# Layer 1's first product for the last 1536 tokens as seven products over halves of tokens

## The chip, the cores and the metric

The kernel runs on one core of a Trainium2 chip. The metric is device microseconds from the start to the end of one execution; lower is better. The matrix engine is TensorE (PE), the vector engine VectorE (DVE), the activation engine ScalarE (ACT); SyncE (SP) issues all DMA transfers, GpSimd (POOL) does next to nothing here. Each engine works through its own instructions in program order and waits on semaphores for the others.

## The reference

Attention with a causal window of 64 keys (4 batches, 8 heads, 576 positions, head size 64), then two layers over the 2304 tokens, 512 wide with 2048 hidden units, all in float32:

```python
scores = scale * np.matmul(q, k.transpose(0, 1, 3, 2))
mask = (rel >= 0) & (rel < window)          # window = 64
scores = np.where(mask, scores, -1000000000.0)
...
attn = attn / (np.sum(attn, axis=-1, keepdims=True) + 1e-09)
x = np.matmul(attn, v)                      # 2304 tokens x 512
h = np.maximum(x @ w_in, 0.0)               # layer 1: 512 x 2048
x = h * h @ w_out                           #          2048 x 512
h = x @ w_in2                               # layer 2
out = (h * np.cos(h)) @ w_out2
```

## The kernel before

Every float32 matrix is split into a high part, rounded to PE's fast 32-bit type (fp32r), and a low part, the rest. Each product is then three matmuls: high by high, high by low, low by high. W1 and W2 arrive as whole float32 numbers ("raw" transfers of 1 MB, one for each slice of 128 hidden units, with the matching rows of w_out) and are unpacked and split on ACT and DVE (`convert_w`, `convert_w2`). The slices of W1 stay in SBUF; those of W2 go to DRAM as w2a, w2b and w2o and are streamed back.

The tokens are cut into nine parts of 256. Attention for a part n and a half of the heads g gives four blocks of matmuls on PE, in this order: scores S (L556), the transposes T (L593, behind mask and minimum on DVE, exp on ACT and the division on DVE), and the product with v, O (L607). From O come the high part of X on ACT (L643) and the low part on DVE (L646).

Layer 1 takes the parts in units: 512 tokens (first in two halves of 256), 256 tokens, and three times 512 tokens. For a unit and a slice of 128 hidden units, `g1` makes the first product, ph: 12 matmuls (four blocks of 128 input columns, three passes) over the unit's tokens. ACT takes relu of it into r, and the square's high part into g; ACT or DVE squares r; DVE takes the low part (L701). `g2` makes the second product from g: 12 matmuls into four accumulators accA (L715), which stay in PSUM over the 16 slices. After the last slice they are copied and stored to DRAM.

Layer 2 takes 768 tokens at a time, and its first product is already made by the scheme that the change brings to layer 1 (Strassen's in Winograd's form): seven products of 6 matmuls over 384 columns in place of eight, in PSUM tiles x, y and z (L997). Its blocks alternate with the second product, accB (L955). `held` is a product copied out by ACT (L1013), which DVE adds to the next (L1020).

The order of the instructions on each engine is not written by hand. Every step is handed to a planner, `op`, with its engines, a key (its place in the program), the steps it depends on, and the buffers that it takes and uses; its modelled duration is also given. The planner runs a list schedule over these numbers and so fixes the order. SP's transfers are such steps too (`dma`), in one queue.

## Time and profile before

| | |
|---|---|
| median of 3 runs | 872.78 us (869.89 to 873.73) |
| profiled execution | 872.92 us |
| its span, first to last instruction | 871.1 us |
| PE, DVE, ACT busy | 847.9, 572.3, 522.9 us |
| moved by DMA | 144.16 MB, mean 165 GB/s |
| mean granted PE clock | 0.992 |

The profile is of one execution, and its span is 1.8 us shorter than the time. A PE matmul is recorded with a modelled end, and matmuls overlap, so the mean duration of a record is longer than the distance between two of them. Weight loads have an engine row of their own, PEld.

### The profile page before, as it was taken

How to read it: one execution, taken by the hardware profiler on the slowest of the kernel's cores; microseconds unless marked ns; L12 is line 12 of the kernel's file. 1: busy time of each engine (PE TensorE's matmuls, PEld its weight loads, DVE VectorE, ACT ScalarE, POOL GpSimd, SP SyncE). 2: the span in 40 equal slices, each digit the busy share in tenths (PEclk: the TensorE clock that was granted, in tenths of full speed). 3: DMA queues.
4: the chain of work that ended last, by engine and by line, in shares of the span. 5: the costliest groups of instructions: out<-in, count | busy, mean ns of one | idle time of the engine just before them, and what ended most of it. 6: DMA issues, size and time to landing. Idle time of an engine off the chain costs nothing.

```text
span 871.1 us, 13901 instructions
## 1 busy us (share of the span) xinstructions
PE 847.9 (97%) x5232; PEld 737.2 (85%) x5232; DVE 572.3 (66%) x1345; ACT 522.9 (60%) x1101; POOL 5.0 (1%) x25
## 2 busy tenths in 40 slices
PE   5799999999999999999999999999999999999998
PEld 4689788998878887888888899988999988999986
DVE  4977855645756366562731588887688877788851
...
DMA packets 28451, 144.16 MB, mean 165 GB/s; under 512 B 3040, under 2 KB 3552, under 8 KB 18144
## 3 DMA queue, kind: packets, MB, share of 16 engines
...
## 4 chain that ended last, share of the span: by engine, by line
PE 91%; DVE 4%; ACT 3%; DMA 1%; issue 0%; ACTq 0%; DVEq 0%
PE accB L955 23%; PE ph L1106 21%; PE accA L715 19%; PE x L997 12%; PE z L997 6%; PE y L997 3%; PE S L556 2%; PE O L607 2%; PE accA L776 2%; PE T L593 2%; ACT pb L575 1%; DMA w2o_dram<-w2o 1%; ACT raw_in_w_dram L286 0%; DVE pb L585 0%; DVE xr L820 0%; DMA qk<-in_qk_dram 0%
## 5 line engine op out<-in xcount | busy, mean ns | idle before, releaser
L1106 PE MATMUL ph<-X,W_in_w_dram 128*128 128x512 f32 (+1 forms) x1032 | 223.0, 363 | 2.7 <-ACT X L643 1.4
L1106 PEld LDWEIGHTS ph<-X,W_in_w_dram 128*128 128x128 f32 x1032 | 173.7, 193 | 32.5 <-issue 1.5
L715 PE MATMUL accA<-g,W_in_w_dram 128*128 128x512 f32 (+1 forms) x888 | 200.2, 370 | 0.2 <-DVE g L701 0.2
L715 PEld LDWEIGHTS accA<-g,W_in_w_dram 128*128 128x128 f32 x888 | 153.4, 189 | 27.6 <-issue 0.7
L701 DVE TENSOR_TENSOR g<-r,g 128x512 fp32r<-128x512 f32 (+1 forms) x86 | 51.8, 603 | 118.1 <-ACT r L696 117.6
L955 PE MATMUL accB<-wo,gb_e 128*128 128x512 f32 x432 | 100.8, 390 | 0.0
L955 PEld LDWEIGHTS accB<-wo,gb_e 128*128 128x128 f32 x432 | 80.9, 188 | 16.2
L692 ACT ACTIVATE g<-r 128x512 fp32r<-128x512 f32 (+1 forms) x86 | 48.2, 561 | 73.2 <-PE accA L715 71.7
L688 ACT ACTIVATE r<-ph 128x512 f32<-128x512 f32 (+1 forms) x86 | 45.1, 524 | 53.6 <-PE ph L1106 51.7
L575 ACT ACTIVATE pb<-pb,mm 128x128 f32<-128x128 f32 x144 | 55.8, 389 | 11.5 <-DVE mm L569 11.4
L955 PE MATMUL accB<-wo,gb_a 128*128 128x512 f32 x216 | 60.8, 394 | 0.0
L955 PE MATMUL accB<-wo,gb_b 128*128 128x512 f32 x216 | 60.6, 393 | 0.0
L696 ACT ACTIVATE r<-r 128x512 f32<-128x512 f32 (+1 forms) x84 | 47.1, 561 | 2.6
L1013 ACT ACTIVATE held<-x 128x384 f32<-128x384 f32 x72 | 34.6, 480 | 20.1 <-PE x L997 20.0
L997 PE MATMUL x<-X,wa 128*128 128x384 f32 x216 | 46.0, 339 | 0.0
L997 PE MATMUL x<-X,wb 128*128 128x384 f32 x216 | 45.5, 336 | 0.0
L955 PEld LDWEIGHTS accB<-wo,gb_b 128*128 128x128 f32 x216 | 39.9, 188 | 5.6
L997 PEld LDWEIGHTS x<-X,wa 128*128 128x128 f32 x216 | 39.0, 188 | 4.5
L955 PEld LDWEIGHTS accB<-wo,gb_a 128*128 128x128 f32 x216 | 39.6, 188 | 3.7
L905 ACT ACTIVATE u_b<-rr_b,hpi 128x384 f32<-128x384 f32 x24 | 14.8, 617 | 44.9 <-DVE rr_b L901 44.8
L997 PEld LDWEIGHTS x<-X,wb 128*128 128x128 f32 x216 | 38.9, 188 | 2.2
L929 DVE TENSOR_TENSOR gb_e<-keep,gb_e 128x384 fp32r<-128x384 f32 x48 | 25.7, 553 | 21.3 <-ACT gb_e L249 21.3
...
## 6 DMA issues: line engine op xcount, KB each, us to landing
raw_in_w_dram<-in_w_dram SPq DMA_DIRECT2D x32, 1024.0 KB, 5.9
wa<-w2a_dram SPq DMA_DIRECT2D x24, 1024.0 KB, 8.2
...
w2o_dram<-w2o SPq DMA_DIRECT2D x8, 1024.0 KB, 4.3
w2a_dram<-w2a SPq DMA_DIRECT2D x8, 1024.0 KB, 4.4
wo<-w2o_dram SPq DMA_DIRECT2D x8, 1024.0 KB, 11.8
```

Source lines behind the costliest of these rows:

```text
L556: nc.tensor.matmul(S[e][HALF[c], r, i], t["qk"][HALF[e], r, q0:q0 + WINDOW], t["qk"][HALF[e], r, UA + q0:UA + q0 + P], start=(r == 0 and i ...
L575: nc.scalar.activation(t["pb"][:, e, r, i], t["pb"][:, e, r, i], AF.Exp, bias=t["mm"][:, e, r, i:i + 1], scale=-1.0, accum_out=t["sm"][:, ...
L688: nc.scalar.activation(t["r"], ph()[:, 0:w], AF.Relu)
L692: nc.scalar.activation(t["g"][:, 0], t["r"], AF.Square)
L696: nc.scalar.activation(t["r"], t["r"], AF.Square)
L701: nc.vector.tensor_tensor(t["g"][:, 1], t["r"], f32(t["g"][:, 0]), ALU.subtract)
L715: nc.tensor.matmul(self.acc[i][:, k, :], w[:, 1, wl, m * P:m * P + P], t["g"][:, gl, :], start=(j == 0 and p == 0 and k == 0 and self.n > ...
L929: nc.vector.tensor_tensor(t["g"][:, 1], r(), f32(t["g"][:, 0]), ALU.subtract)
L955: nc.tensor.matmul(acc[0], t["g"][:, gl, m * P:m * P + P], wb.tile[:, k % 2, wl], start=(k == 0 and i == 0), stop=(k == NJ - 1 and i == 2))
L997: nc.tensor.matmul(ps[bank], wb.tile[:, i, wl, c * P:c * P + P], piece(o, c, xl), start=(first and c == 0 and k == 0), stop=(last and c == ...
L1013: return b, op({"ACT": act_us(H)}, key - 6, lambda e: nc.scalar.activation(r_at(b), ps[bank], AF.Copy), [dep, o_rooms], [b], [buf], lat=0.39)
L1106: nc.tensor.matmul(t["ph"][:, 0:u.w], wb.tile[:, 0, wl, c * P:c * P + P], u.x(xl, c), start=(c == 0 and k == 0), stop=(c == NCC - 1 and k ...
```

## The change

For the last three units (1536 tokens) the first product is no longer made slice by slice. The tokens of a unit are halved (256 and 256), the 512 input columns are halved, and two slices of 128 hidden units form the two halves of the output: a 2 by 2 by 2 block product, made by seven products of 6 matmuls over 256 columns (`group1`). The order in a group is B11 into x, B21 into y, T2 into x, T1 into the other half of y, T3 into x, T4 into x, B22 into y. Between them stand the eight blocks of three matmuls of 512 columns (`tiles1`) that make the second product of the group before: one behind y, one behind T2, two behind T3, four behind B22. ACT copies x out three times (`hold`, r1 to r3); DVE makes the sums o_11, o_22 and o_12 (`add`); o_21 is a copy on ACT. `act1` then makes relu and square in one DVE operation for both tokens' halves of a slice, the high part on ACT, the low part on DVE.

The seven sums of X for a unit are made by `prepare1`: four differences, seven high parts (ACT or DVE) and seven low parts (DVE), all of 512 columns. The seven pieces have one buffer each and are written again for the next unit. The attention of these units leaves O as a plain float32 copy. The seven weight matrices of each pair of slices are made by `sum_w1` when W1 is unpacked, and stored to DRAM as w1s (1.84 MB for a pair); each group loads its pair again (`load_in1`, in two transfers, w_in), issued when the group two before has ended. A slice of W1 is now split with two operations of 512 columns on each engine and not one of 1024. The conversions of W2 move: four slices behind `sum_w1`, then two with each of the groups 1, 4, 7, 11, 14 and 18. Layer 2's first loads wait for the last load of w_in. In the planner the price of a DMA byte, and for parts from 2 on those of the mask step and of exp, are lower.

```diff
-        return op({"SP": max(0.6 * n, nbytes / 360e3)}, key, fn, [*deps, *order], take, use, lat=2.2)
+        return op({"SP": max(0.6 * n, nbytes / 400e3)}, key, fn, [*deps, *order], take, use, lat=2.2)
...
+            hi = op({"ACT": act_us(DM)}, key, c5, [o4, w_hi[j - 1][k] if q else None],
+                    [] if q else [wb], [rb, wb] if q else [rb])
+            his.append(hi)
+            los.append(op({"DVE": dve_us(DM)}, key, c6, [hi], use=[rb, wb]))
+        w_hi[j], w_lo[j] = his, los
...
+    def sum_w1(i, key, after):
...
+        def s1(e):
+            t["s"] = wp.tile([P, 4, 2, Q], F32R, tag=f"W{sb.slot}", name=f"w1s_{i}")
+            nc.vector.tensor_tensor(raw(1), part(1, 0), part(1, 1), ALU.add)
...
+        def s2(e):
+            nc.vector.tensor_tensor(raw(0), raw(1), part(0, 0), ALU.subtract)
...
+        def s3(e):
+            nc.vector.tensor_tensor(raw(2), part(0, 0), part(1, 0), ALU.subtract)
...
+        def s4(e):
+            nc.vector.tensor_tensor(raw(3), part(0, 1), raw(0), ALU.subtract)
...
+        def lo(e):
+            nc.vector.tensor_tensor(
+                t["s"][:, :, 1], f32(t["s"][:, :, 1]), f32(t["s"][:, :, 0]), ALU.subtract)
...
+        o = op({"DVE": dve_us(2 * DM)}, key, whole, [*ready, after, *cv_last], [ab], [wb])
+        o = op({"DVE": dve_us(Q)}, key, s1, [o], [sb], [ab])
+        o = op({"DVE": dve_us(Q)}, key, s2, [o], use=[ab, sb])
+        o = op({"DVE": dve_us(Q)}, key, s3, [o], use=[ab, sb])
+        o = op({"DVE": dve_us(Q)}, key, s4, [o], use=[ab, sb])
+        cv_last[:] = [o]
+        o = op({"ACT": act_us(4 * Q)}, key, hi, [o], use=[sb])
+        o = op({"DVE": dve_us(4 * Q)}, key, lo, [o], use=[sb])
...
+        w1_stored[i] = [
+            dma(key, whole_st, P * 4 * Q * 4, [*ready, after], use=[wb], n=2),
+            dma(key, st22, P * 2 * Q * 4, [*ready, after], use=[wb]),
+            dma(key, st_a, P * 6 * Q * 4, [o], use=[sb]),
+            dma(key, st_b, P * 2 * Q * 4, [o], use=[sb])]
...
-                    prev = op({"DVE": 0.36}, k_e, lambda q, e=e, r=r, i=i: neg_max(q, e, r, i),
+                    prev = op({"DVE": 0.36 if n < 2 else 0.22}, k_e, lambda q, e=e, r=r, i=i: neg_max(q, e, r, i),
...
-                    ex.append(op({"ACT": 0.59}, k_e, lambda q, e=e, r=r, i=i: exp(q, e, r, i),
+                    ex.append(op({"ACT": 0.59 if n < 2 else 0.39}, k_e, lambda q, e=e, r=r, i=i: exp(q, e, r, i),
...
+            def raw(eng):
...
+                copy(eng, rx(g, th), t["O"].rearrange("p r q -> p (r q)"))
...
+    def prepare1(u, key):
...
+        def sub(dst, a, b, deps):
+            return op({"DVE": dve_us(2 * UA)}, key, lambda e: nc.vector.tensor_tensor(
+                dst(), a(), b(), ALU.subtract), deps, use=d)
...
+        x11, x12, x21, x22 = at(0, 0), at(0, 1), at(1, 0), at(1, 1)
+        a = split1(u, B11, x11, [got[0, 0]], key, d, free(B11))
+        b = split1(u, B21, x21, [got[1, 0]], key, d, free(B21))
+        t1 = sub(x11, x12, x11, [*a, got[0, 1]])
+        s1 = split1(u, T1, x11, [t1], key, d, free(T1))
+        t3 = sub(x12, x22, x12, [t1, got[1, 1]])
+        s3 = split1(u, T3, x12, [t3], key, d, free(T3))
+        s5 = split1(u, B22, x22, [got[1, 1]], key, d, free(B22))
+        t2 = sub(x22, x22, x11, [t1, t3, *s5])
+        s2 = split1(u, T2, x22, [t2], key, d, free(T2))
+        t4 = sub(x21, x21, x22, [t2, *b])
+        s4 = split1(u, T4, x21, [t4], key, d, free(T4))
...
+        def sq(e):
+            nc.vector.scalar_tensor_tensor(r["r"], r["r"], 0.0, r["r"], ALU.max, ALU.mult)
...
+        o = op({"DVE": dve_us(512)}, key, sq, ready, use=[rb[0]])
+        h = op({"ACT": act_us(512)}, key, hi, [o], [gb], [rb[0]])
+        l = op({"DVE": dve_us(512)}, key, lo, [h], use=[rb[0], gb])
...
+    def load_in1(u, i, key, after):
...
+                nc.sync.dma_start(f32(b.tile[:, 0:n]), w1s[i][:, a:a + n])
+
+            o = dma(key, ld, P * n * 2 * Q1 * 4, [*w1_stored[i], *after],
+                    [b, slot] if fresh else [b], [] if fresh else [slot])
...
+    def group1(u, i, key, fill):
...
+        gaps = [[], fill[0:1], fill[1:2], fill[2:4], fill[4:]]
...
+                    for n, (wl, xl) in enumerate(((0, 0), (0, 1), (1, 0))):
+                        nc.tensor.matmul(
+                            out(), wb.tile[:, k, wl, c * P:c * P + P],
+                            piece1(o, xl)[:, c * UA:c * UA + UA],
+                            start=(new and n == 0), stop=(last and c == 1 and n == 2),
...
+
+                line[0] = op({"PE": 3 * pe_us(UA)}, key, mm,
+                             [line[0], o_w, *ready1[u, o], *(deps if c == 0 else ())],
+                             [buf] if new else [], [wb, *s_buf] if new else [wb, buf, *s_buf],
...
+        def hold(dep):
+            b = R["R1"].buf()
+            return b, op({"ACT": act_us(UA)}, key - 6, lambda e: nc.scalar.activation(
+                r_at(b), ps["x"], AF.Copy), [dep], [b], [bx, rr_buf], lat=0.39)
...
+        def add(k, h, r, deps):
+            first = not rows[k][0].users
+            return op({"DVE": dve_us(UA)}, key - 6, lambda e: nc.vector.tensor_tensor(
+                new_r(k)[:, h * UA:(h + 1) * UA], ps["y"][:, h], r_at(r), ALU.add), deps,
+                [rows[k][0]] if first else [], [by, r, rr_buf] + ([] if first else [rows[k][0]]))
...
+        nm = f"{u}_{i}"
+        o = product(0, pa, 0, B11, True, True)
+        r1, o_r1 = hold(o)
+        o = product(1, pa, 1, B21, True, True)
+        o_11 = add(0, 0, r1, [o, o_r1])
+        between()
+        between()
+        o = product(0, pa, 2, T2, False, True, [o_r1])
+        r2, o_r2 = hold(o)
+        between()
+        oz = product(2, pa, 3, T1, True, True, [o_11])
+        o = product(0, pb, 0, T3, False, True, [o_r2])
+        r3, o_r3 = hold(o)
+        o_22 = add(1, 1, r3, [oz, o_r3])
+        between()
+        o = product(0, pb, 1, T4, False, True, [o_r3])
+        o_21 = op({"ACT": act_us(UA)}, key - 3, lambda e: nc.scalar.activation(
+            new_r(1)[:, 0:UA], ps["x"], AF.Copy), [o, o_22], use=[bx, rows[1][0]])
+        gb = act1(key - 3.0, rows[1], [o_22, o_21], f"{nm}b")
+        o = product(2, pb, 2, B22, False, True, [o_22])
+        o_12 = add(0, 1, r2, [o, o_r2, o_11])
+        ga = act1(key - 2.9, rows[0], [o_11, o_12], f"{nm}a")
+        between()
+        return ga, gb
...
+        ends = []
+        for i in range(NJP):
...
+            load_in1(u, i, key - 7.0, ends1[-2:-1])
+            if u * NJP + i in (1, 4, 7, 11, 14, 18):
+                for _ in range(2):
+                    convert_w2(w2_next, key + 8.0, line[0])
+                    w2_next += 1
+            ga, gb = group1(u, i, key, fill)
+            ends1.append(line[0])
+            fill = [*tiles1(u, 2 * i + 1, key + 2.0, gb, i == 0, False, ends),
+                    *tiles1(u, 2 * i, key + 2.0, ga, False, i == NJP - 1, ends)]
+        if u + 1 < NU1:
+            prepare1(u + 1, base1 + 2.0 * (u + 1) * NJP - 2.0)
```

The first place where the order moves is PE's row at the start of the first group. Names are tile<-tiles read: X is the split input, g the split square, accA_0 the accumulators of the 256-token unit ahead. Before, the next unit's products of 512 columns begin between the last second products of that unit:

```order
L715 MATMUL accA_0_1697<-g_2250,W_in_w_dram_1075 128x256 x6
L715 MATMUL accA_1_1733<-g_2250,W_in_w_dram_1075 128x256 x6
L1106 MATMUL ph_2321<-X,W_in_w_dram_370 128x512 x12
L715 MATMUL accA_0_1697<-g_2281,W_in_w_dram_1165 128x256 x6
...
L715 MATMUL accA_0_1697<-g_2325,W_in_w_dram_1229 128x256 x6
L715 MATMUL accA_1_1733<-g_2325,W_in_w_dram_1229 128x256 x6
...
L1106 MATMUL ph_2418<-X,W_in_w_dram_430 128x512 x12
L715 MATMUL accA_0_2449<-g_2355,W_in_w_dram_370 128x512 x3
```

After the change the seven products stand there; between the first y and T2 lie half a fill and eight rows of S, of which one is shown:

```order
L820 MATMUL accA_0_1818<-g_2378,W_6_1136 128x256 x6
L820 MATMUL accA_1_1831<-g_2378,W_6_1136 128x256 x6
L1431 MATMUL x_0_0_2455<-X,w_in_0_0_1674 128x256 x6
L1431 MATMUL y_0_0_2466<-X,w_in_0_0_1674 128x256 x6
L820 MATMUL accA_0_1818<-g_2410,W_7_1247 128x256 x3
L648 MATMUL S_0_0_2481<-qk_0_2039 64x128 x2
...
L1431 MATMUL x_0_0_2455<-X,w_in_0_0_1674 128x256 x6
L820 MATMUL accA_0_1818<-g_2410,W_7_1247 128x256 x3
L1431 MATMUL y_0_0_2466<-X,w_in_0_0_1674 128x256 x6
L1431 MATMUL x_0_0_2455<-X,w_in_0_4_1946 128x256 x6
L820 MATMUL accA_1_1831<-g_2410,W_7_1247 128x256 x6
L1431 MATMUL x_0_0_2455<-X,w_in_0_4_1946 128x256 x6
```

The first product of the unit, ph with 12 matmuls of 512 columns, has given way to x and y with 6 of 256; T2 is the third product row (the second x), T1 the second y, and the second products of the 256-token unit are now the fills.

The second place is DVE just ahead of it. held_1741 and x_raw hold the plain O of the four quarters of X, w2o, w2a and w2b are W2's sums. Before, the low part of X came straight from O, and this stretch had no such rows. After:

```order
L806 TENSOR_TENSOR g_2378<-r_2359,g_2378 128x256
L258 CAST w2o_2357<-cw_in_w_dram_2364 128x512
L428 TENSOR_TENSOR w2o_2357<-cw_in_w_dram_2364,w2o_2357 128x512
...
L428 TENSOR_TENSOR w2b_2422<-cw_in_w_dram_2326,cw_in_w_dram_2364 128x256
L806 TENSOR_TENSOR g_2410<-r_2395,g_2410 128x256
...
L428 TENSOR_TENSOR w2a_2408<-w2a_2408 128x2x256
L927 TENSOR_TENSOR X<-held_1741,X 128x512
L948 TENSOR_TENSOR held_1741<-held_1741,x_raw 128x512
L258 CAST X<-held_1741 128x512
L927 TENSOR_TENSOR X<-held_1741,X 128x512
...
L927 TENSOR_TENSOR X<-held_1741,X 128x512
L1462 TENSOR_TENSOR r_0_0_0_2510<-y_0_0_2466,held_1741 128x256
```

Between the split g_2378, which PE reads ahead of the group, and the low part of T2 (the second row with L927) stand the conversion of a pair of W2's slices, another split of a square, and the difference T2 = x22 - x11 (L948); o_11 (L1462) comes behind the pieces of T4.

The third place is SP in the first groups. Before, the queue held raw slices, q/k, v and the stores of W2's sums:

```order
L275 DMA raw_in_w_dram_3459<-in_w_dram 128x2048
L541 DMA v_1_3494<-in_v_dram 128x1024
L537 DMA qk_0_3544<-in_qk_dram 128x1152
L275 DMA raw_in_w_dram_3596<-in_w_dram 128x2048
L541 DMA v_0_3664<-in_v_dram 128x1024
L372 DMA w2o_dram<-w2o_3547 128x2048
```

After, the pairs of loads of w_in stand between them:

```order
L1370 DMA w_in_0_0_1674<-w1s_dram 128x2048
L1370 DMA w_in_0_4_1946<-w1s_dram 128x1536
L629 DMA qk_0_2938<-in_qk_dram 128x1152
L278 DMA raw_in_w_dram_2954<-in_w_dram 128x2048
L278 DMA raw_in_w_dram_2975<-in_w_dram 128x2048
L1370 DMA w_in_1_0_2075<-w1s_dram 128x2048
L1370 DMA w_in_1_4_2211<-w1s_dram 128x1536
L633 DMA v_0_3071<-in_v_dram 128x1024
L629 DMA qk_1_3090<-in_qk_dram 128x1152
L446 DMA w2o_dram<-w2o_3130 128x2048
L1370 DMA w_in_0_0_1674<-w1s_dram 128x2048
L1370 DMA w_in_0_4_1946<-w1s_dram 128x1536
```

Each pair of loads that moved in is 1.05 and 0.79 MB, and is queued behind the raw slices, q/k, v and stores ahead of it.

## Rows read from the trace of the kernel before

**Rows 1.** The page, busy time of each engine (share of the span), instructions:

```profile
PE 847.9 (97%) x5232; PEld 737.2 (85%) x5232; DVE 572.3 (66%) x1345; ACT 522.9 (60%) x1101; POOL 5.0 (1%) x25
```

**Rows 2.** Waits of PE, whole run: total us, times, longest.

```profile
PE T L593 <- DVE pb L585: 5.2, 5, 2.9
PE T L593 <- ACT pb L575: 4.7, 3, 2.3
PE S L556 <- DMA qk<-in_qk_dram: 4.5, 1, 4.5
```

**Rows 3.** Waits of PE from 50 us to the end.

```profile
PE T L593 <- DVE pb L585: 0.4, 2, 0.2
PE accA L715 <- DVE g L701: 0.2, 1, 0.2
```

**Rows 4.** Windows: us, each engine's busy time, granted PE clock, DMA share, GB/s.

```profile
core 0: us, PE busy (x) PEld busy (x) DVE busy (x) ACT busy (x) POOL busy (x), PEclk, DMA share, GB/s
15.60:49.70 34.10, 25.17 (x277) 21.29 (x278) 28.16 (x73) 29.04 (x65) 0.00 (x0) 0.87 0.86 346
...
111.00:198.60 87.60, 87.37 (x813) 78.76 (x812) 50.37 (x155) 57.03 (x157) 0.00 (x0) 1.00 0.42 153
198.60:486.20 287.60, 287.44 (x1728) 234.49 (x1728) 147.24 (x379) 165.31 (x349) 0.00 (x0) 1.00 0.47 176
505.00:520.00 15.00, 15.00 (x79) 13.93 (x78) 12.43 (x27) 9.42 (x18) 0.00 (x0) 1.00 1.02 425
510.00:579.00 69.00, 69.00 (x361) 64.15 (x360) 59.96 (x128) 41.40 (x80) 0.00 (x0) 1.00 0.51 207
```

**Rows 5.** Groups by line and shape: busy us, mean ns of a record.

```profile
L1106 PE MATMUL ph<-X,W_in_w_dram 128*128 128x512 f32 x696 | 173.3, 395 | 0.0
...
L1106 PE MATMUL ph<-X,W_in_w_dram 128*128 128x256 f32 x336 | 49.7, 297 | 2.7 <-ACT X L643 1.4 <-ACT r L688 1.0 <-DVE X L646 0.3
...
L1013 ACT ACTIVATE held<-x 128x384 f32<-128x384 f32 x72 | 34.6, 480 | 20.1 <-PE x L997 20.0
```

**Rows 6.** Chain that ended last, from 440 us: start, us, what.

```profile
442.87 2.72 PE ph L1106 x12
```

**Rows 7.** The same chain, 60 to 90 us.

```profile
64.81 1.44 PE ph L1106 x12
...
80.51 2.75 PE ph L1106 x12
83.26 1.43 PE accA L776 x12
```

**Rows 8.** The same chain in layer 2, from 506 us.

```profile
506.00 1.39 PE accB L955 x6
507.39 1.04 PE x L997 x6
...
517.55 1.39 PE accB L955 x6
```

**Rows 9.** DVE in time, from 202 us: start, us, instruction.

```profile
202.28 0.42 DVE L354 TENSOR_TENSOR w2b<-cw_in_w_dram,cw_in_w_dram 128x256 f32<-128x256 f32 x1 [1.97 <-DMA w2o_dram<-w2o]
202.62 0.42 DVE L354 TENSOR_TENSOR w2b<-cw_in_w_dram,w2a 128x256 f32<-128x256 f32 x1
...
204.35 0.68 DVE L701 TENSOR_TENSOR g<-r,g 128x512 fp32r<-128x512 f32 x1
204.95 0.68 DVE L354 TENSOR_TENSOR w2b<-w2b 128x512 fp32r<-128x512 f32 x1
```

**Rows 10.** DVE groups by shape: the split of a W1 slice.

```profile
L324 DVE TENSOR_TENSOR W_in_w_dram<-raw_in_w_dram,W_in_w_dram 128x1024 fp32r<-128x1024 f32 x16 | 19.6, 1223 | 7.8 <-ACT W_in_w_dram L249 7.6
```

**Rows 11.** The chain from 198 us: the block S.

```profile
206.95 1.03 PE S L556 x32
```

**Rows 12.** DMA issues from 505 to 520 us: count, KB each, median us to landing.

```profile
wa<-w2a_dram SPq DMA_DIRECT2D x3, 1024.0 KB, 19.8
```

**Rows 13.** Window from 60 to 70 us, columns as in Rows 4.

```profile
60.00:70.00 10.00, 10.00 (x86) 10.00 (x85) 7.99 (x10) 9.90 (x17) 0.00 (x0) 1.00 0.25 79
```

More of the change, by code (lines that the diff above doesn't have):

```diff
@@ L672, in x @@
         def x(self, hl, c):
-            return X[:, self.half, hl, c, self.sl]
+            return (x_first() if self.n == 0 else x_third())[:, hl, c]
         def x_ready(self, c):
@@ L1182 @@
     for jp in range(2):
[L1183 to L1189 removed]
+        load_in(0, jp, base - 8.0 + 2.0 * jp, [*loaded, *w2_end])
+    load_out(0, base - 7.0, [*loaded, *w2_end])
+    gate = loaded[0]
+    fills = [fill[0:4], fill[4:8]]
     job_ends = []
```

322 lines of the change are left out of this document (249 added, 73 removed).

## The prediction

> **What bounds the kernel now.** I read the busy times first. TensorE (PE) is busy 847.9 of 871.1 us [rows 1], so the reader is to see that only two things can move the time: the work that PE has, and the 23 us in which it waits. The waits come next: three kinds, 14.4 us together, stand in the attention of the start [rows 2], and of all waits only 0.6 us lie behind 50 us [rows 3]. From there PE works without a break, and the time is the sum of its matmuls. Then the stretches [rows 4]: while W1 is unpacked (15.6 to 49.7 us) PE has work for 25.17 of 34.10 us; in the stretch of the units of 512 tokens that the change rewrites (198.6 to 486.2 us) PE is busy 287.44 of 287.60, VectorE (DVE) 147.24, ScalarE (ACT) 165.31, and the DMA engines 0.47 of the time. Last the chain that ended last, for the price of a matmul: mean durations of single records overlap (395 ns for 512 columns, 297 for 256 [rows 5]) and are no price, but a run of 12 in the chain is.
>
> **Removed.** Three units of 512 tokens, 16 slices, 12 matmuls of 512 columns: 576 matmuls. Twelve take 2.72 us [rows 6], 0.2267 each: 130.56 us.
>
> **Added on PE.** 24 groups (three units, eight pairs of slices) of 7 products with 6 matmuls of 256 columns: 1008 matmuls. Twelve of 256 columns take 1.44 us [rows 7], 0.120 each: 120.96 us. So PE has 9.60 us less. The price is not quite half of 0.2267 because both hold about 13 ns that do not shrink with the columns (0.2267 = a + 512b, 0.120 = a + 256b); the seven-eighths that the scheme promises (16.3 us) are not to be had.
>
> A page of the Trainium skill speaks against the change here: "TensorE: Matmul & The Clock Gate", section "Back-to-back issue gap", gives for a stream of loads and matmuls about 81 ns at 128 columns and 131 ns at 512. An estimate on a line between them is 98 ns at 256, and by it 1008 x 0.098 - 576 x 0.131 = 23 us more work, not 9.6 less. This case's rows, 0.120 against 0.2267, disagree, and the rows decide.
>
> **Switches.** Where blocks of unlike matmuls alternate, 12 of 512 take 2.75 in place of 2.72, while the 256-column block behind them takes 1.43 in place of 1.44 [rows 7]: 0.02 for a pair of switches. The second layer already runs this pattern. Its group goes from 506.00 to 517.55, 11.55 us; 42 matmuls of 384 columns at 1.04 for six and 18 of 512 at 0.2267 make 11.36, so 0.19 for five fills, 0.04 each [rows 8]. The new group has four fills: 24 x 4 x 0.02 = 1.9 us, bounds 0 and 24 x 4 x 0.04 = 3.8. I take 1.9, since the pair 512 and 256 is the nearer row. A group is then 10.48 + 0.08 = 10.56 us against 10.88 for two slices before.
>
> **Inside a steady group: nothing.** Each new step on ACT and DVE (three holds, three adds, a copy, two squares, two splits) has PE work in front of its reader. The hold of the first product is followed by y (0.72) and a fill (0.68), 1.40 us, before T2 overwrites x; a hold of 384 columns took 0.48 us in layer 2 [rows 5], where the same scheme with the heavier activation keeps DVE busy 59.96 and ACT 41.40 of 69.00 us while PE does 69.00 [rows 4]. The new group asks for 3 adds of 256 and 4 operations of 512 on DVE, start to start 0.34 and 0.60 us [rows 9]: 3.4 us of 10.56. If that cover were gone at one hand-over, the price would be some 0.3 us x 24 = 7 us.
>
> **The sums of weights and of X: nothing in the stretch before.** `sum_w1` costs DVE per pair two operations of 1024 columns (1.22 us, the nearest row [rows 10]) and four of 256: 3.8 us, 30 us for eight; `prepare1` some 7. On top of 50.37 of 87.60 us between 111 and 198.6 [rows 4] that makes 88 by busy times; these overlap, start to start is 0.60 for 0.69 [rows 9], so about 77. Full, but not over. Cutting the conversion of a W1 slice in halves adds 2 x 0.69 - 1.22 = 0.16 us on DVE and as much on ACT at most, 16 times, half of them in the stretch to 49.7 where PE waits anyway [rows 4]. The planner's shorter numbers for the mask and exp steps shift rows in the attention too. The bounds for the start are -2 to +2 us; I take 0, since the waits there are on a chain of attention steps that stays the same.
>
> **The way into the first group: 2 us.** In the order of after, the DVE rows from the split of `g_2378` to the low part of T2 are 13: six of 512 columns and of 2x256 at 0.60, two casts at 0.4, five of 256 at 0.34 = 6.1 us [rows 9]. PE has in that time the second product with `g_2378` (1.44), x and y (0.72 each), half a fill (0.36) and S (1.03 [rows 11]): 4.3 us. T2 thus comes 1.8 us late if PE takes `g_2378` as it appears, 0.6 if it was 1.2 ahead. T1's product waits for `o_11`, which is queued on DVE behind the difference and split of T4, for some tenths more. Sum 1 to 3, taken as 2. Behind the waiting matmul everything on PE waits, and nobody makes it good later.
>
> **Later ways in.** At the two changes of unit the X pieces are written again: some eight operations of 512 columns on DVE at 0.60, 4.8 to 4.9 us, up to T2's low part, while PE has five fills (0.68), x and y (0.72): 4.84 us. 0 to 0.5 each, taken as 0.3 for both. Into layer 2, 0.1 to 0.6, taken as 0.2. T's of the attention, now planned with less room: 28 of them at 0 to 0.1, taken as 0.5 in all. Sum 1.0, bounds 0 to 4.4.
>
> **DMA: nothing, but near.** Each group loads 1.05 + 0.79 MB, 44.0 MB in all; the stretch moved 176 GB/s x 287.6 us = 50.6 MB before. 94.6 MB in 283 us is 334 GB/s. At a share of 1.02 the engines moved 425 GB/s [rows 4], at 0.47 176 (374 at a full share). So 79 to 89% of what they can do. A load is issued at the end of group k-2 and wanted at the start of group k, one group of 10.6 to 11.7 us ahead.
>
> **Sum.** 872.92 - 9.60 + 1.9 + 0 + 2 + 1.0 = **868.2 us**, against the profiled execution, which lies 0.14 us above the median of 872.78. With every unknown at its better end: 872.92 - 9.60 + 0 - 2 + 1 + 0 = 862.3; at its worse end 872.92 - 9.60 + 3.8 + 2 + 3 + 4.4 = 876.5.
>
> **Rivals.**
> *Slower: the W1 sums come late.* SP issues transfers in order, and two raw slices (1 MB each), a q/k, a v and the stores of w2 stand between the w_in rows. A load that finds the queues full took 19.8 us to land in layer 2 [rows 12], which is more than the one group of lead here. It decides when the DMA engines give less than 94.6 MB in 292 us, 324 GB/s: then the stretch is 9 us longer than forecast and the time above 877.3. At 315 GB/s it is 300 us and 885. For it: that landing time and a nearly full share. Against it: in layer 2, where the share is 1.02, PE does not wait (15.00 of 15.00 [rows 4]); the bytes between two loads are at most 5.2 MB, 12.5 us at 420 GB/s.
> *No change that can be told.* The hand-overs cost 0.2 us in each group, or both unit changes and the T's go to their worse ends: 868.2 + 4 to 5 = 872 to 873. For it: the DVE chains at the ways in are as long as PE's cover. Against it: layer 2.
> *More gain.* No stall at the ways in and a start that gets ahead: 862 to 864.
> *DVE is the bound before the first group.* If 88, not 77, of 87.6 us count, the second products wait for their low parts: +1 to +8 us, 869 to 876.
> *A part of each matmul that does not shrink.* If 256 columns cost in this place what their records' means say, 297/395 of 0.2267 = 0.170 us, 1008 of them take 171.8 us, 41 more than the 130.56 removed: 914 with nothing else; weight loads that the shorter matmul no longer covers would do it. Against it: with 256-column matmuls PE did its 86 matmuls from 60 to 70 us in 10.00 us [rows 13], though the weight loads were busy all 10.00. The page named above tells this case, and its estimate is 23 us; the trace has not borne it out.
>
> **Chances.** The forecast with its bounds (864 to 872) 0.54; more gain 0.12; no change with 872 to 877 0.12; late loads 0.15; DVE 0.05; the fixed part 0.02. A difference under 0.5%, 4.4 us, is not to be told from none in this kernel, so "faster" ends at 868.4. Of the forecast's 0.54 some 0.35 lie below that: faster 0.12 + 0.35 + 0.01 = 0.48; slower 0.15 + 0.02 + 0.01 = 0.18; same 0.34. The range is 861 to 879: below is 0.04, above about 0.13, most of it the late loads.
>
> **What would show it.** A chain of groups with 10.56 us of x, y and accS (more in groups with S, T and O); 0.72 for six of 256; a wait of T2's first matmul on DVE of 1 to 2 us in front of the first group, once; waits of PE on the transfer of w_in nowhere. The prediction is wrong if PE waits for w_in in several groups, if a switch costs 0.05 or more, if DVE's holds recur as PE waits in each group, or if PE's waits before 50 us change by more than 2 us.

## The result and the profile after

The changed kernel takes 883.12 us (median of 4 runs, 882.76 to 884.06) against 873.0 before: 1.0124 of it, 95% interval 1.0099 to 1.015. That is 10 us slower where 4.7 less were forecast, and outside the range.

Four marks cut both profiles in stretches of equal work on PE: the first product of 512 columns of the first unit, the first product of the last three units, layer 2's first product, the end.

| stretch, us | before | after | forecast |
|---|---|---|---|
| start, to the first 512-column product | 76.2 | 74.6 | 76.2 |
| then to the last three units | 122.4 | 130.7 | 122.4 |
| the last three units ("groups") | 287.6 | 289.6 | 282.7 |
| layer 2 | 384.9 | 386.3 | 385.1 |
| span | 871.1 | 881.2 | 866.4 |

(Of the forecast, the 9.60 less, the 1.9 and 2.8 of the 3.0 us of waits are put into the groups, 0.2 into layer 2; each row is of one profiled execution.) The page of the changed kernel, busy time, and the windows of its last three stretches, columns as in [rows 4]:

```profile
PE 844.7 (96%) x5664; PEld 751.9 (85%) x5664; DVE 663.5 (75%) x1539; ACT 522.2 (59%) x1157; POOL 5.0 (1%) x25
```

```profile
74.59:205.31 130.72, 124.88 (x1058) 108.17 (x1057) 101.21 (x260) 98.01 (x233) 0.00 (x0) 0.99 0.66 233
205.31:494.86 289.55, 282.44 (x2163) 249.06 (x2162) 212.39 (x513) 160.02 (x383) 0.00 (x0) 1.00 0.86 332
494.86:881.20 386.34, 381.95 (x1897) 343.13 (x1895) 298.01 (x627) 203.71 (x398) 0.00 (x0) 1.00 0.38 145
```

Of the first of these windows [rows 4] holds the last 87.6 us; whole, before, it was

```profile
76.17:198.60 122.43, 122.05 (x1059) 106.84 (x1058) 80.19 (x220) 90.34 (x218) 0.00 (x0) 1.00 0.37 133
```

so 122.05 us of work for PE in 122.43; now it has 124.88 in 130.72. It stands idle for 5.8 us in place of 0.4, and its busy time rose by 2.8 us, about half of it at one place at a lower clock (below). The second had 287.44 in 287.60 [rows 4] and has 282.44 in 289.55: PE's work fell by 5.0 us, and it stands idle for 7.1 in place of 0.2. So in both most of the loss is waiting. What it waits for from 50 us on, where [rows 3] were all there was:

```profile
PE T L685 <- DVE pb L677: 4.8, 5, 2.0
PE y L1431 <- DVE r L1462: 2.9, 5, 1.0
PE x L1431 <- DVE X L927: 1.4, 2, 1.1
PE T L685 <- ACT pb L667: 1.1, 1, 1.1
PE y L1431 <- ACT r L793: 1.0, 1, 1.0
PE x L1431 <- ACT held L1449: 0.7, 1, 0.7
```

**What was right.** A steady group, in the chain (start, us, what), goes from 438.85 to 449.46, 10.6 us, and the next two take 10.5 each; 10.56 were forecast. Its seven products are the blocks of 0.71 and 0.72:

```profile
438.85 2.75 PE accS L1389 x12
441.60 0.71 PE x L1431 x6
442.31 0.72 PE y L1431 x6
443.03 0.70 PE accS L1389 x3
...
449.46 2.75 PE accS L1389 x12
```

And w_in never holds PE: no wait on it is in the list.

**The stretch ahead of the groups.** DVE in time, in it (start, us, instruction; in brackets its idle time before and what ended it):

```profile
128.45 1.22 DVE L349 TENSOR_TENSOR w<-W 128x1024 f32<-128x1024 f32 x1
132.00 0.43 DVE L360 TENSOR_TENSOR w1s<-w 128x256 f32<-128x256 f32 x1 [2.33 <-DMA w1s_dram<-w1s]
...
140.22 0.69 DVE L677 TENSOR_TENSOR pb<-pb,sm 128x512 f32<-128x512 f32 x1
...
155.12 0.43 DVE L360 TENSOR_TENSOR w1s<-w 128x256 f32<-128x256 f32 x1 [2.58 <-DMA w1s_dram<-w1s]
...
161.29 0.69 DVE L677 TENSOR_TENSOR pb<-pb,sm 128x512 f32<-128x512 f32 x1
```

PE at the same places:

```profile
141.06 0.63 PE L685 MATMUL T<-ident,pb 128*128 128x128 f32 x4 [1.90 <-DVE pb L677]
...
162.13 0.63 PE L685 MATMUL T<-ident,pb 128*128 128x128 f32 x4 [2.05 <-DVE pb L677]
```

`sum_w1`'s next sum (L360) writes into the buffer from which the last sum is still being stored, so it waits for the DMA, and DVE's row behind it waits with it: the attention's division (L677) comes late, and PE stands before T for 1.90 and 2.05 us. The windows around show what the DMA engines do at that time, and PE's granted clock behind both waits:

```profile
141.00:146.00 5.00, 4.84 (x54) 4.29 (x56) 4.70 (x11) 3.88 (x10) 0.00 (x0) 1.00 1.06 392
145.00:160.00 15.00, 15.00 (x148) 13.23 (x146) 8.43 (x29) 8.06 (x19) 0.00 (x0) 1.00 1.01 362
162.13:168.00 5.87, 5.87 (x37) 5.87 (x38) 5.18 (x11) 4.20 (x14) 0.00 (x0) 0.71 0.65 224
168.00:180.00 12.00, 11.76 (x143) 11.08 (x142) 10.77 (x37) 8.76 (x30) 0.00 (x0) 1.00 0.90 298
```

The DMA engines are full from 140 to 160 us (share 1.01; before, from 111 to 198.6 us, they were at 0.42 [rows 4]). Behind the first wait the granted clock stays at 1.00. Behind the second it is 0.71 for 5.9 us, part of that time at the lower of its two levels (1.2 for 2.4 GHz), and then 1.00 again. In the chain, twelve matmuls of 256 columns there against twelve later:

```profile
163.12 2.38 PE ph L1279 x12
165.50 1.99 PE accA L820 x12
...
184.72 1.44 PE ph L1279 x12
```

2.38 and 1.99 in place of 1.44: behind the wait of 2.05 us the lower clock costs 1.5 us more. The next longest waits of T, at 96 and 98 us (1.1 and 0.3 us), lie ahead of these stores. With the planner's old numbers (e3, below) the second is gone and the first is 0.8; what is left of the first, 0.7 us or more in every run, stays open.

**The groups.** First the way in, PE in time:

```profile
207.22 0.98 PE L1431 MATMUL y<-X,w_in 128*128 128x256 f32 x6 [1.02 <-ACT r L793]
...
209.86 0.35 PE L1431 MATMUL x<-X,w_in 128*128 128x256 f32 x1 [0.27 <-DVE X L258]
210.49 0.85 PE L1431 MATMUL x<-X,w_in 128*128 128x256 f32 x5 [0.28 <-DVE X L927]
...
212.69 0.98 PE L1431 MATMUL y<-X,w_in 128*128 128x256 f32 x6 [0.99 <-DVE r L1462]
```

2.6 us, about as forecast, but split otherwise: T2 (the second x) waits 0.55 us and T1 (the second y) 0.99, and the other 1.02 are a wait of the first y on ACT, which had itself stood before one of W2's sums on DVE:

```profile
205.74 0.63 ACT L254 ACTIVATE w2a<-w2a 128x512 fp32r<-128x512 f32 x1 [1.04 <-DVE w2a L428]
```

Then ACT at 330 us and PE behind it:

```profile
332.94 1.11 ACT L289 ACTIVATE raw_in_w_dram<-raw_in_w_dram 128x1024 f32<-128x1024 f32 x1 [2.38 <-DMA raw_in_w_dram<-in_w_dram]
333.95 0.37 ACT L1449 ACTIVATE held<-x 128x256 f32<-128x256 f32 x1
```

```profile
334.37 0.98 PE L1431 MATMUL x<-X,w_in 128*128 128x256 f32 x6 [0.65 <-ACT held L1449]
...
337.02 0.97 PE L1431 MATMUL y<-X,w_in 128*128 128x256 f32 x6 [0.97 <-DVE r L1462]
```

ACT stands 2.38 us before a raw slice of W2 that has not landed. The hold (L1449) is queued behind it, and PE's x (T2 or T3 overwrite what is held) and then y, whose sum comes late, wait. In the groups' window a raw slice takes a median of 11.7 us to land and the loads of w_in 8.5; in the same stretch before, in the last line, a raw slice took 5.5:

```profile
w_in<-w1s_dram SPq DMA_DIRECT2D x22, 1024.0 KB, 8.5
...
raw_in_w_dram<-in_w_dram SPq DMA_DIRECT2D x14, 1024.0 KB, 11.7
```

```profile
raw_in_w_dram<-in_w_dram SPq DMA_DIRECT2D x12, 1024.0 KB, 5.5
```

### The profile page after: what moved, and what is told of

Its sections match the earlier page's. It is cut to its first block, busy times and chain, and to the rows that moved or that the text cites. A ratio compares the mean times of both kernels' runs of the same rounds, so it can differ in the third digit from the quotient of the medians.

```text
span 881.2 us, 15176 instructions
## 1 busy us (share of the span) xinstructions
PE 844.7 (96%) x5664; PEld 751.9 (85%) x5664; DVE 663.5 (75%) x1539; ACT 522.2 (59%) x1157; POOL 5.0 (1%) x25
## 4 chain that ended last, share of the span: by engine, by line
PE 66%; DVE 13%; ACT 9%; DMA 9%; issue 3%; SPq 0%; DVEq 0%; ACTq 0%
PE accB L1135 23%; PE x L1177 11%; PE accS L1389 8%; DMA raw_in_w_dram<-in_w_dram 6%; PE z L1177 6%; PE x L1431 4%; PE y L1431 3%; PE y L1177 3%; PE ph L1279 3%; PE accA L820 2%; DMA w1s_dram<-w1s 2%; ACT raw_in_w_dram L254 2%; ACT raw_in_w_dram L289 2%; PE T L685 1%; ACT W L254 1%
## 5 line engine op out<-in xcount | busy, mean ns | idle before, releaser
L1431 PE MATMUL x<-X,w_in 128*128 128x256 f32 x576 | 86.8, 286 | 2.5 <-DVE X L927 1.4
L1431 PEld LDWEIGHTS x<-X,w_in 128*128 128x128 f32 x576 | 78.5, 190 | 9.7 <-ACT held L1449 1.9
L1279 PE MATMUL ph<-X,W 128*128 128x256 f32 (+1 forms) x456 | 81.7, 327 | 0.0
L1279 PEld LDWEIGHTS ph<-X,W 128*128 128x128 f32 x456 | 67.2, 200 | 5.7 <-issue 0.9
L1431 PE MATMUL y<-X,w_in 128*128 128x256 f32 x432 | 66.7, 287 | 4.2 <-DVE r L1462 2.9
L1431 PEld LDWEIGHTS y<-X,w_in 128*128 128x128 f32 x432 | 58.5, 190 | 8.8 <-DVE r L1462 5.4
L667 ACT ACTIVATE pb<-pb,mm 128x128 f32<-128x128 f32 x144 | 55.9, 391 | 14.7 <-DVE mm L661 14.4
L820 PE MATMUL accA<-g,W 128*128 128x256 f32 (+1 forms) x312 | 57.2, 329 | 0.1
L820 PEld LDWEIGHTS accA<-g,W 128*128 128x128 f32 x312 | 47.6, 193 | 5.4 <-DVE g L806 0.5
L1462 DVE TENSOR_TENSOR r<-y,held 128x256 f32<-128x256 f32 x72 | 30.2, 420 | 25.9 <-ACT held L1449 25.3
L1339 DVE SCALAR_TENSOR_TENSOR r<-r 128x512 f32<-128x512 f32 x48 | 32.8, 689 | 21.6 <-ACT r L1482 21.0
L1449 ACT ACTIVATE held<-x 128x256 f32<-128x256 f32 x72 | 27.1, 376 | 33.8 <-PE x L1431 33.2
```

What stands on the lines that cost most here:

```text
L667: nc.scalar.activation(t["pb"][:, e, r, i], t["pb"][:, e, r, i], AF.Exp, bias=t["mm"][:, e, r, i:i + 1], scale=-1.0, accum_out=t["sm"][:, ...
L820: nc.tensor.matmul(self.acc[i][:, k, :], w[:, wl, m * P:m * P + P], t["g"][:, gl, :], start=(j == 0 and p == 0 and k == 0 and self.n > 0), ...
L1279: nc.tensor.matmul(t["ph"][:, 0:u.w], wb.tile[:, j % 2, wl, c * P:c * P + P], u.x(xl, c), start=(c == 0 and k == 0), stop=(c == NCC - 1 an ...
L1339: nc.vector.scalar_tensor_tensor(r["r"], r["r"], 0.0, r["r"], ALU.max, ALU.mult)
L1431: nc.tensor.matmul(out(), wb.tile[:, k, wl, c * P:c * P + P], piece1(o, xl)[:, c * UA:c * UA + UA], start=(new and n == 0), stop=(last and ...
L1449: return b, op({"ACT": act_us(UA)}, key - 6, lambda e: nc.scalar.activation(r_at(b), ps["x"], AF.Copy), [dep], [b], [bx, rr_buf], lat=0.39)
```

## The experiments

**The theory** after the result: the bytes of the change make transfers late, and engines that work in order stand at them; stores of w1s ahead of the groups ("store theory"), raw slices in the groups ("load theory"). **Rivals:** the work that the sums add on DVE; the planner's shorter numbers for the mask and exp steps; DVE's own chains at the changes of unit. Where stretches are named, they are those of the table, measured with the same marks in one profiled execution. The rounds ran on several chips, on which the kernel before took 871.1 to 872.2 us in the median (873.0 in the result), so a time is best read by its ratio to the kernel before on the same chip; the changed kernel's is 1.0124 (1.0099 to 1.015). The program fixes its order anew for each edit that changes a planned step, and the order alone moves a stretch too: in e10 below, the groups, which its edit does not touch, take 286.1 us and not 289.6. Only e4 and e6 run in the order of the changed kernel; e6's groups take 288.6 us, so a stretch of one execution is good to 1 us or so.

### The stretch ahead of the groups

**Early stores** (e1). The stores that need no sum lose their dependence on the last split and get an earlier key:

```diff
-            dma(key, whole_st, P * 4 * Q * 4, [*ready, after], use=[wb], n=2),
-            dma(key, st22, P * 2 * Q * 4, [*ready, after], use=[wb]),
+            dma(8.0 * i, whole_st, P * 4 * Q * 4, ready, use=[wb], n=2),
+            dma(8.0 * i, st22, P * 2 * Q * 4, ready, use=[wb]),
```

> The two stores of a pair of W1 slices that need no sums (0.79 MB of 1.84) are issued as soon as the pair is split, in the stretch from 50 to 112 us where the DMA engines are 0.31 busy, and not after the last split. Store theory: sum_w1's next sum waits for the store of the sum before it, and DVE's queue behind it holds the attention's division; with 6.3 MB out of the way the DVE waits on w1s stores fall from 5.1 us to under 2, the two waits of T (1.90 and 2.05 us) and the clock's fall behind the second go, and the time falls by 4 to 7 us, to 876 to 879. Rival, DVE work: the 30 us of sums that stand ahead of the division are the same, so T waits as before and the time stays at 883 +- 1.5. Rival, planner's numbers: the same, no change.

Measured: 879.17 us, ratio 1.0086 (1.0068 to 1.0104). The stretch is 124.2 us for 130.7, T's waits behind 100 us are gone, DVE's wait on w1s is 0.3 us, and from 145 to 160 us the DMA engines are 0.47 busy in place of 1.01. With the new order some of DVE's work also moved behind the mark: it is busy 95.1 us in the stretch for 101.2; the next run tells whether that matters. The groups took 295.1 us in the profiled execution, 5.5 more, which no theory had said: ACT stands before raw slices for 11.6 us in place of 6.6, and PE before two holds for 2.60 and 2.38 us, each followed by a few microseconds at a lower clock. That execution took 881.77 us, the other three 878.8 to 879.3, so the loss is smaller as a rule.

**No low parts of the sums** (e10): the operation `lo` of `sum_w1` is left out.

```diff
         o = op({"ACT": act_us(4 * Q)}, key, hi, [o], use=[sb])
-        o = op({"DVE": dve_us(4 * Q)}, key, lo, [o], use=[sb])
```

> The operation that makes the low parts of the W1 sums (1024 columns on DVE, 1.14 us, eight times) is left out, so the stored low parts hold the whole sums; stores move the same bytes. DVE work theory: 9 us of DVE work fewer in the stretch of 130.7 us to the first group, T's waits there (5.6 us) halve and the stretch falls by 2 to 4 us. Store theory: the next sum waits for the store as before (DVE's wait on w1s 5 us or more, as it arrives earlier), T's waits stay above 4 us, the stretch stays within 1.5 us.

Measured, in one execution: 881.32 us; the stretch is 132.9 us (PE's mean clock in it is 0.97 for 0.99), DVE's busy time in it 94.69 and not 101.21, and it waits longer on the stores, 6.2 us. With as little work on DVE as in e1 and the stores where they were, the stretch gained nothing; the work theory falls. The stretch in e1, then in e10, columns as in [rows 4]:

```profile
74.40:198.64 124.24, 122.67 (x1059) 106.29 (x1058) 95.08 (x249) 96.22 (x232) 0.00 (x0) 1.00 0.65 225
```

```profile
74.29:207.21 132.92, 125.62 (x1059) 109.28 (x1058) 94.69 (x256) 98.87 (x237) 0.00 (x0) 0.97 0.68 233
```

DVE's wait on the stores in e10:

```profile
DVE w1s L360 <- DMA w1s_dram<-w1s: 6.2, 3, 3.1
```

**Whole sum on GpSimd** (e2):

```diff
-        o = op({"DVE": dve_us(2 * DM)}, key, whole, [*ready, after, *cv_last], [ab], [wb])
+        o = op({"POOL": pool_us(2 * DM, True)}, key, whole, [*ready, after, *cv_last], [ab], [wb])
```

> The first sum of sum_w1 (high plus low part of W1, 1024 columns) is made by GpSimd, which does nothing here, and no longer by DVE; stores and their waits stay. DVE work theory: DVE is relieved of 8 x 1.14 = 9 us between 112 and 205 us, T's waits of 1.90 and 2.05 us shrink by about 1 us each, and the time falls by 2 to 4 us. Store theory: the sums behind it still wait for the store of the sum before, so DVE's waits on w1s remain above 4 us and the time moves by less than 1.5 us either way.

Measured: 886.16 us, ratio 1.016; the stretch is 133.1. Neither theory had this. DVE's busy time rose, to 104.74 us, with 9 us of its work gone: a subtraction of 512 columns beside a GpSimd sum takes 2.58 us and not 0.69. GpSimd first, then DVE, in time:

```profile
131.02 2.40 POOL L349 TENSOR_TENSOR w<-W 128x1024 f32<-128x1024 f32 x1 [6.92 <-DVE w1s L369]
```

```profile
131.39 2.58 DVE L806 TENSOR_TENSOR g<-r,g 128x512 fp32r<-128x512 f32 x1 [0.54 <-ACT r L801]
```

So the run doesn't separate the theories; e10 does. The Trainium skill, "SBUF — State Buffer", section "SBUF: two separate sides", says that DVE and GpSimd share one pair of ports, which one instruction locks whole while the other stands. The rows agree: DVE's subtraction, 0.69 us long elsewhere, ends 0.55 us behind GpSimd's sum.

**Whole rows** (e6): one store of 4 KB rows for two in pieces of 1 KB (and the matching index in `product`).

```diff
-            for a in range(2):
-                nc.sync.dma_start(
-                    w1s[i][:, a], f32(wb.tile[:, 0, :, a * Q:(a + 1) * Q]))
+            nc.sync.dma_start(
+                w1s[i][:, 0:2], f32(wb.tile[:, 0].rearrange("p l (a n) -> p l a n", a=2)))
```

> The high and low part of the first slice of a pair are stored as whole rows of 4 KB in one transfer, in place of two transfers in pieces of 1 KB; the products read the same matrices at other places. The stores move the same bytes. If the pieces are what makes the stores late, DVE's waits on w1s (5.1 us) fall to 2 us or less and the stretch from the first 512-column product to the first group (130.7 us) falls by 3 to 5 us. If it is the bytes, it stays within 1.5 us.

Measured, in one execution: 881.53 us, the stretch 130.2, DVE's wait 4.5. It is not the pieces; that the bytes at that time matter is shown by e1.

**Store planned late** (e12): the program is told that the stores of the sums take longer, and orders DVE's row by it.

```diff
-            dma(key, st_a, P * 6 * Q * 4, [o], use=[sb]),
-            dma(key, st_b, P * 2 * Q * 4, [o], use=[sb])]
+            dma(key, st_a, P * 6 * Q * 4, [o], use=[sb], lat=7.0),
+            dma(key, st_b, P * 2 * Q * 4, [o], use=[sb], lat=7.0)]
```

> The planner takes 7 us and not 2.2 for the stores of the W1 sums; the program does the same work and moves the same bytes. Store theory (the next sum stands too early in DVE's row, and the attention's division is queued behind its wait): DVE's wait on w1s falls from 5.1 to under 1.5 us, T's waits after 88 us fall from 5.6 to under 2 us, the stretch to the first group falls from 130.7 to 124 to 127 us; the groups stay at 288 to 291; time 877 to 880. DVE work theory: same work, the stretch stays within 1.5 us.

Measured: 882.55 us, ratio 1.0127, no gain. DVE's wait is 0.8 us, as the store theory says, but the stretch is 129.0 us, and one wait of T of 3.48 us is left at 161 us. ACT and PE there:

```profile
157.56 0.60 ACT L840 ACTIVATE x<-accA 128x512 f32<-128x512 f32 x1 [4.17 <-DMA x_dram<-x]
```

```profile
161.45 1.09 PE L685 MATMUL T<-ident,pb 128*128 128x128 f32 x4 [3.48 <-ACT r L801]
```

The same full DMA queue comes through another door: the first unit's result (x_dram) is stored behind the W1 stores, ACT waits 4.17 us for that buffer, and exp is queued behind. In the changed kernel ACT stands at that place for a sum of DVE (2.29 us), and this copy starts at 157.75 us, nearly the same time. So the theory holds in a wider form, late stores of any kind, and the size it gave for this door alone was too large.

**Old numbers** (e3):

```diff
-                    prev = op({"DVE": 0.36 if n < 2 else 0.22}, k_e, lambda q, e=e, r=r, i=i: neg_max(q, e, r, i),
+                    prev = op({"DVE": 0.36}, k_e, lambda q, e=e, r=r, i=i: neg_max(q, e, r, i),
...
-                    ex.append(op({"ACT": 0.59 if n < 2 else 0.39}, k_e, lambda q, e=e, r=r, i=i: exp(q, e, r, i),
+                    ex.append(op({"ACT": 0.59}, k_e, lambda q, e=e, r=r, i=i: exp(q, e, r, i),
```

> The planner's numbers for the mask step and exp are those of before for all parts (0.36 and 0.59 in place of 0.22 and 0.39), all else as in the changed kernel. Planner's numbers theory: T's waits after 50 us (5.9 us) fall below 1 us, since the plan leaves more room, and the time falls by 4 us or more. Store theory: the delay is not in these steps; the waits of DVE on w1s stores stay near 5 us and T's waits fall by 2 us at most; the 1.6 us that the start gained may be lost again: 881 to 885.

Measured: 878.39 us, ratio 1.0078 (1.0057 to 1.0098); in the profiled execution, the fastest of four (875.56), stretch 126.7, groups 286.9, DVE's wait on w1s 2.7 us, T's waits 1.1 us: partly as each said. The old numbers leave room ahead of T; the late store shows as a wait of S on ACT instead (2.2 us, ACT behind x_dram for 5.3 us). **Both together** (e15, e12's and e3's edits):

> The stores of the W1 sums planned with 7 us, and the old numbers of the mask step and exp. If both act on T's waits by the same way, the stretch to the first group is no shorter than with the better of the two alone (126.7 us with the old numbers); if they add up, 123 to 125 us. Groups as with the old numbers, 286 to 288 us. Time 873 to 877.

Measured: 879.97 us, ratio 1.0111, above the time expected; 127.4 and 287.8: they don't add up, and what is left is again one wait of S, 3.0 us at 160 us, behind x_dram. Both only move the row away from a late transfer; only the early stores make it less late.

### The groups

**Small loads** (e4):

```diff
-                nc.sync.dma_start(f32(b.tile[:, 0:n]), w1s[i][:, a:a + n])
+                m = n if fresh else 1
+                nc.sync.dma_start(f32(b.tile[:, 0:m]), w1s[i][:, a:a + m])
```

> Of the seven weight matrices of a pair only one of each transfer is loaded from the third group on, 0.52 MB a group in place of 1.84 (29 MB less; products then take an older pair's matrices). Load theory: in the stretch of the groups the transfers of raw W2 slices come late (11.7 us to landing, 5.5 before), ACT and DVE stand at them in order with the holds and sums queued behind; with the loads cut, raw lands in about 6 us, the waits at 334, 337, 341 and 411 us (3.0 us) go, and the stretch from 205 to 495 us falls by 3 to 5 us. Rival, chains: the waits in the stretch are DVE's own chains at the changes of unit; then 411 us and the way in stay and the stretch falls by under 1.5 us.

Measured: 879.38 us, ratio 1.0076 (1.0059 to 1.0092); the order is that of the changed kernel. Groups 285.7, 3.8 less; no wait of ACT on raw is left, and of PE's waits those of the way in (2.6 us), 1.09 at 408 us and 0.42 at 488. The load theory holds; the wait at the second change of unit (411 us, here 408) is DVE's chain, as the rival says.

**Raw planned late** (e5): 9 us and not 2.2 for raw slices of W2, `lat=9.0 if keep else 2.2` in their load.

> The planner takes 9 us and not 2.2 for the way of a raw W2 slice behind its issue; nothing else is changed. Load theory: ACT's waits on raw in the stretch of the groups (6.6 us) fall below 2 us, as the steps on it now stand later in ACT's row, the holds behind them are free, PE's waits at 334 to 341 us (1.9 us) go; stretch of the groups 287 to 288 us for 289.6, time 880 to 882. Rival, chains of DVE: no change of the stretch by more than 0.7 us.

Measured: 880.77 us, ratio 1.0109 (1.0085 to 1.0132), which is not clear of the changed kernel's; groups 286.2, and ACT waits on raw nowhere. That is 3.4 us less, nearly what cutting 29 MB gave, by the order alone, but not in the same waits: those at 334 to 341 us (1.9 us) are gone as expected, at the way in 1.9 us went too, and the second change of unit waits 2.67 us for 1.09. Layer 2 takes 1.5 us more (387.9).

**W2 later** (e8): no slices ahead of the groups, pairs in more of the groups.

```diff
-            while w2_next < 4:
+            while w2_next < 0:
...
-            if u * NJP + i in (1, 4, 7, 11, 14, 18):
+            if u * NJP + i in (1, 3, 5, 8, 11, 14, 16, 18):
```

> The first four W2 slices are no longer converted ahead of the first group but with groups 1 and 3, and the others move behind them. Chain theory of the way in: the DVE rows of w2o, w2a and w2b ahead of T2 are gone, PE's waits from 207 to 213 us (2.6 us) fall to 1 us or less. They come back as traffic of raw slices in the groups: the waits on holds there rise by 1 to 4 us, so the time is 881 to 885. If the waits from 207 to 213 us stay, they come from the chain of X alone.

Measured, in one execution: 881.09 us; no wait is left at the way in, so it came from W2's rows on DVE; the groups are 289.6 as in the changed kernel, with ACT's waits on raw at 9.7 us.

### Both at once

**e7**: the edits of e1, e5 and e3.

> Early stores, raw W2 planned with 9 us, and the old numbers of mask step and exp together. If the three theories hold and add up: first stretch 124 us (as with early stores), group stretch 285.5 to 287 us (hold waits of ACT on raw gone, way in and changes of unit left), layer 2 386.3: span 870 to 873, time 872 to 875. If the early stores only pass their delay on to the groups, the group stretch is above 291 us again and the time is 876 or more.

Measured: 882.94 us, ratio 1.0133, a clear miss: 124.0, but 295.2 in the groups. One wait of 6.03 us of PE's x on DVE's X at 406 us: a W2 pair now fell into the change of unit, and its rows stand on DVE ahead of T2.

**e13**: e15 with raw planned at 6 us, and the pairs moved:

```diff
-            if u * NJP + i in (1, 4, 7, 11, 14, 18):
+            if u * NJP + i in (1, 4, 9, 12, 17, 19):
```

> As the run with late stores and old numbers, and besides the raw W2 slices planned with 6 us and their pairs asked for with groups 1, 4, 9, 12, 17 and 19, so that no conversion falls into a change of unit. Load theory: hold waits of ACT on raw under 2 us and no wait above 1 us at the changes of unit: group stretch 284 to 286 us, time 870 to 873, level with the kernel before. Rival: late pairs push layer 2's first loads back, and what the groups gain is lost at its start (386 to 389 us).

Measured: 876.0 us, ratio 1.0053 (1.0035 to 1.0071); groups 284.3, the least of all; 128.0 ahead of them (S behind x_dram, 3.5 us), layer 2 387.6. The length of the groups came out as expected, though one wait of 1.69 us is left at the first change of unit; the rest did not.

**f7**: e1 and the pairs moved.

> Early stores, and the pairs of W2 slices asked for with groups 1, 4, 9, 12, 17 and 19 in place of 1, 4, 7, 11, 14 and 18. First stretch 124 us as with early stores. If the place of the pairs is what the early stores pass their delay to, the group stretch falls from 295 to 288 us or less; if it is the planned time of the raw transfers, it stays above 291 us.

Measured: 881.41 us, ratio 1.0123; groups 294.9, ACT's waits on raw 12.2 us. The place of the pairs is not it. **f1**: the same with raw planned at 6 us.

> As the run before, and the raw W2 slices planned with 6 us. If order and planned time are all, both cures hold at once: first stretch 124 to 125 us, group stretch 284 to 286 us, layer 2 386 to 388 us, time 870 to 874, level with the kernel before. If the bytes set it, the group stretch stays above 289 us and the time at 875 or more.

Measured: 874.41 us (10 runs), ratio 1.0034 (1.002 to 1.0048): 124.2 and 287.6 us, ACT's waits on raw 1.3 us. Of the 1.24% 0.9 are back, by order and planned times alone; the groups are 2 us above what was expected. **f9**: f7 with raw at 9 us and the old numbers.

> Early stores, pairs spread, raw planned with 9 us, old numbers of mask step and exp. Where that kernel without the spread had 295.2 us in the groups, 6.0 of them one wait at the second change of unit behind a W2 pair: with no pair there that wait is under 2 us and the group stretch 285 to 289 us; first stretch 124 us; time 871 to 876. If the wait at the change stays above 4 us, the chain of X is its own cause.

Measured: 884.78 us, ratio 1.0155. The wait at the change is gone (0.43), but W2 is now stored so late that layer 2 waits for it:

```profile
496.83 2.26 PE L1178 MATMUL x<-x_more,wa 128*128 128x384 f32 x6 [10.74 <-DMA wa<-w2a_dram]
```

**f13**: f1 with the loads of e4.

> The kernel with early stores, spread pairs and raw planned with 6 us, and from the third group on only one of the seven weight matrices of each transfer is loaded, 0.52 MB a group in place of 1.84 (products then take an older pair's matrices). Load theory: the waits on q/k and on holds in the groups go and the stretch is 284 to 285 us, the time 870 to 872, at or just below the kernel before. Chains: it stays at 287 us and the time at 874.

Measured: 874.55 us, groups 286.0. The next run has the same 286.0 with the full loads, so the load theory falls for what is left: it is not the loads. **f12**: f1 with the rows of e6.

> The same kernel with full loads, and the first slice of a pair stored as whole rows of 4 KB in one transfer. The early stores are out of the way already, so the first stretch stays at 124 us and the time within 1 us of 874.4. If the pieces of 1 KB delay the start or the raw loads of W1, the time falls by 1 to 2 us, level with the kernel before.

Measured: 873.92 us (12 runs), ratio 1.0026 (1.0014 to 1.0037), the best version with the full work, and still not below the kernel before. Its windows of the same stretches:

```profile
73.99:198.35 124.36, 122.71 (x1058) 106.28 (x1057) 95.32 (x250) 95.38 (x231) 0.00 (x0) 1.00 0.65 226
198.35:484.36 286.01, 281.46 (x2162) 248.90 (x2161) 220.23 (x528) 160.43 (x381) 0.00 (x0) 1.00 0.86 330
484.36:871.70 387.34, 382.37 (x1897) 342.96 (x1895) 297.49 (x626) 204.39 (x399) 0.00 (x0) 1.00 0.40 153
```

## Why the prediction was wrong, point by point

- **Removed and added matmuls, switches:** right in a steady group (10.5 for 10.56 us). Over the groups PE's busy time fell by 5.0 us and, where few waits are left (e5, f12), by 6.0, not the 7.7 of the sum; where the other 1.7 us go was not traced.
- **"Inside a steady group: nothing."** Nearly right for the hand-overs themselves: in f12 PE's waits on sums, splits and holds are 2.9 us in all 24 groups. Wrong in what else stands in ACT's row: a hold is only as early as the raw slice ahead of it. 3.8 us (e4).
- **"The sums of weights and of X: nothing in the stretch before."** The step that failed: 8.3 us. It counted DVE's work, which is not the bound (e10), and not the store that must end before the next sum. The store is shown as the cause by e1 and e10 together: with 6.3 of the 14.7 MB stored earlier the stretch takes 6.5 us less, and with as little of DVE's work in it but the stores left where they were it takes no less. The rival that DVE is the bound there had the place and nearly the size (1 to 8 us), and the wrong cause. 1.5 us are the clock behind one wait. The loss shows at T, for which the sum had only 0.5 us, and for another reason (less room in the plan): T waits 5.9 us, 5.6 of them in this stretch.
- **The way in: 2 us.** 2.6, and from the rows named, W2's on DVE (e8); but T2's own wait is 0.55 us where 1.8 was worked out, and 1.0 us came by way of ACT, which the sum did not have, so that the size fits is partly luck. **Later ways in:** 1.1 us at the second change, 0.3 at the first; layer 2 takes 1.4 us more where 0.2 was forecast, 0.7 of it waits.
- **"DMA: nothing, but near."** Wrong, and the rival looked at the wrong transfer: w_in, double-buffered, never held PE. That the measured time lies where this rival put it (above 877.3 us) is chance. Its point of decision, a mean under 324 GB/s, failed too: the groups ran at 332 and were late, since what counts is how long one raw slice takes to land, 11.7 us for 5.5, against the 4.8 or so that the planner gives it (1.05 MB at 400 GB/s and 2.2 us).
- **The start:** 1.6 us better, within its bounds. **The rule of the Trainium skill** ("TensorE: Matmul & The Clock Gate", "Back-to-back issue gap"): not borne out by this trace; six of 256 columns take 0.71 to 0.72 us, 0.12 each, beside the 98 ns estimated on a line between its figures, and PE's work in the groups fell by 5.0 us where that estimate would have it rise by 23.

So the seven products do save PE work, 6.0 us over the groups where 7.7 was forecast, and the transfers that the scheme needs take back more than that, ahead of the groups and in them. With the transfers cured the kernel comes within 0.3% of the one before. What f12 still loses is 4.5 us of idle time in the groups (2.2 of it waits of y for DVE's sums), 2 us ahead of the groups and 2.4 us in layer 2's stretch. Whether another order takes that away was not tried.

## What to carry to other kernels

Price a scheme that saves matmuls by the bytes it adds, stretch by stretch, and ask of each transfer which in-order engine stands at it and what is queued behind: a store that frees a buffer counts as much as a load. A mean DMA rate below the peak doesn't make a transfer hidden; compare its time to land under that load with the time that the order allows for it. Where a planner fixes the order, its latencies are such claims. To correct one gave nearly as much here as to cut the bytes (3.4 and 3.8 us in the groups), and with it the moved work can collide with the next stage (f9).

## What had not been expected

A DVE operation with two inputs took 2.58 us for 0.69 beside a GpSimd sum (e2), so an idle GpSimd was no free place for DVE's work. A single wait of PE of 2.05 us was followed by 5.9 us at a granted clock of 0.71, while one of 1.90 us, 21 us earlier, was followed by none; in e4, where that earlier wait is 2.54 us, the clock behind it is 0.67 to 143 us and 0.66 to 146. And cutting 29 MB of loads, or only planning the raw slices later, brought the groups to nearly the same length, 285.7 and 286.2 us.
